# Split transfers, optional zero products and a new step order in an RWKV chunk kernel with a token mixer behind it

## Chip, core and metric

The kernel runs on one core of one Trainium2 chip. Its time is that of one execution on the device in microseconds (us). The core has five engines that run side by side: TensorE (PE in the profile, with its weight loads as PEld) multiplies matrices into PSUM, VectorE (DVE), ScalarE (ACT) and GpSimd (POOL) work on elements, and SyncE (SP) issues transfers. Sixteen DMA engines move the data. POOL does not read PSUM in this kernel; what TensorE makes is taken out by DVE or ACT.

## What is computed

Inputs are r, k, v, w with 4 batches, 8 heads, 768 tokens and 48 channels, u with 8 × 48, and three weight matrices; all in float32. Only the core of the reference is shown:

```python
for t in range(S):                                     # S = 768
    cur = einsum('bhd,bhe->bhde', u[None] * k_t, v_t)
    y[:, :, t] = einsum('bhd,bhde->bhe', r_t, state + cur)
    state = w_t[:, :, :, None] * state + einsum('bhd,bhe->bhde', k_t, v_t)
x = y.transpose(0, 2, 1, 3).reshape(B, S, 384)
W_tok = (1 / 8) * einsum('bsd,btd->bst', x @ w_q, x @ w_k)
out = maximum(einsum('bst,btd->bsd', W_tok, x), 0) @ w_out
```

## The kernel before

The 768 tokens of a batch are three *units* of 256 tokens, each of two chunks (c = 0, 1) of 128. Twelve units, n = 0 to 11, are worked through in turn, three to a batch. Within a chunk the recurrence is written as matrix products. The steps of one unit and their names, which are also tile names in the profile:

- loads of w, k, r, v into wg, kg, rg, vg (rings of four buffers each, 384 KB a load, lines 231 to 240). For the last batch v comes in four pieces vw (line 242).
- **ln** (line 406, ACT): the logarithm of w, into lw. **cw** (line 429, TensorE): its running sums, 16 products with CM. **ep**, **en** (lines 445 and 453, ACT): the exponentials of the sums and of their negatives.
- **k16**, **r16**, **v16** (line 412): casts to bf16, on POOL, ACT or DVE. **kT**, **rT** (line 466, TensorE): their transposes. **ks** (line 501): k out of PSUM. **qT**, **RT** (DVE), **KT** (POOL or DVE; line 519): products with each other and with the exponentials.
- **vp**, **VB** (line 547): v in the chunk order, out of PSUM. **dps**, **dd**, **Vd** (lines 561 to 580): the term with u.
- **A** (line 587, TensorE): the 128 × 128 blocks of all heads of a chunk; **AM** (line 594, DVE): the same with the mask US.
- **kb**, **kd** (lines 602 and 615), **sn**, **SB** (lines 636 to 660): the state. **yi**, **ya** (lines 669 and 680, TensorE) and **X** (line 708, DVE): the output rows.
- **xt**, **XT**, **qk**, **QK**: X transposed and multiplied with w_q and w_k.

After the third unit of a batch come **T**, **TS** (line 791), and for each block of 256 tokens **mx** (line 807), **rl** (the maximum with 0), **fp** (line 825, the product with w_out), **os** (out of PSUM) and **st** (the store, line 840). In unit 0, and at the end, some steps go by single chunks.

`setup` (line 248) clears and builds the constants, with nine products of a zero tile Z on TensorE. `pads` (line 295) clears each of the two kd buffers once. `bonus` (line 374) prepares u: cast uC, transpose uT, copy UB. WARM = 12 (line 139) further products of Z, named z, stand among the steps.

The order is a list: `ORDER` (line 80) names all steps by number, `WAYS` names the engine of each step that has a choice (E, e, c TensorE, the small letters in another form of the same step; A ACT; D, d DVE; P POOL; S SP), and `BANKS` the PSUM bank of each PSUM buffer. The steps are issued in that order; every engine, SP too, takes its own in the order in which they stand, and waits where an operand or a buffer is not ready. The steps named Q and L (line 348, "wire" and "land") have no function and issue nothing.

Of the kernel before, what the change touches and what calls it, by code (L numbers as in the profile page):

```python
# [32 lines left out]
class Plan:  # L33

    ENGINE = dict(E="E", e="E", c="E", A="A", D="D", d="D", P="P", S="S", Q="Q", L="L")

    def __init__(self):
        self.steps = []  # L40
# [20 lines left out]
    def order(self):  # L61
        ways = iter(WAYS)
        for s in self.steps:
            if len(s["ways"]) > 1:
                s["way"] = next(ways)
                assert s["way"] in s["ways"], s["key"]
            s["eng"] = self.ENGINE[s["way"]]
        for b, x in zip(self.banks, BANKS):
            b.bank = x
        assert sorted(ORDER) == list(range(len(self.steps)))  # L70
        done = []
        for i in ORDER:
            s = self.steps[i]
            assert all(x["out"] for x in s["after"]), s["key"]
            if s["buf"] is not None and s["buf"].kind == "x":
                s["buf"].kind = "s" if s["way"] == "E" else "w"
            s["out"] = True
            done.append(s)
        return done


ORDER = [
# [40 lines left out]
]  # L123
WAYS = (
    "PDDDAPPDDdPADPPDDEEEAAPPAdPAAPEAcEEAAPPAPPADPeDEEDAAAAAAAAPPDPDADPeAcEEDAPPAdPAAPEAEEEDA"
    "PPDPPAAPeAEEAAAAAAAAAAPDPPAAPEDEcEAAPPDPPDAPEAEEEAAPPDPPAAPeDceAAAAADADDPAAPPAPEDcEEDAPP"
    "DPPAPeAcceAAPPDPPPAPPAEEDDAEDADAAADAAAADADDA"
)
BANKS = [
# [6 lines left out]
]  # L136


WARM = 12


@with_exitstack
def kernel(
# [12 lines left out]
    nc = tc.nc  # L156
    B, H, S, D = r.shape
# [70 lines left out]
    gv = const([C, 1], F32, "gv")  # L228
    gk = const([C, 1], F32, "gk")

    def load(b, i, tl, ap):
        nc.sync.dma_start(
            out=view(tl, 0, [[D2, H], [1, D2]]),
            in_=ap[b, :, ds(i * U, U)].rearrange("h (p j) d -> p h (j d)", j=2))

    def load_long(b, i, tl, ap):
        nc.sync.dma_start(
            out=view(tl, 0, [[2 * D2, NP], [1, 2 * D2]]),
            in_=dataclasses.replace(ap, offset=(b * H * S + i * U) * D,
                                    ap=[[4 * D, 64], [S * D, H], [1, 4 * D]]))  # L240

    def load_whole(b, q, tl):
        nc.sync.dma_start(
# [102 lines left out]
    wts = {}  # L346

    def dma(key, fn, after=(), buf=None, reads=()):
        x = add(key, "S", fn, after, buf)
        y = add(key + ("wire",), "Q", None, [x])  # L350
        return add(key + ("land",), "L", None, [y], reads=reads)

    def weights():
        def f_qk(e):
# [27 lines left out]
    def unit(n, batch):  # L382
# [9 lines left out]
        for name, ap in (("wg", w), ("kg", k), ("rg", r)) + (() if whole else (("vg", v),)):  # L392
            f = load_long if name in ("kg", "rg") and long else load
            g[name] = ring(name)
            g[name + "L"] = dma((name, n), lambda e, ap=ap, f=f, x=g[name].tile: f(b, i, x, ap),
                                buf=g[name])
            if n == 0 and name == "wg":
                bonus(g["wgL"])
# [404 lines left out]
        for ii in range(NU):  # L803
# [34 lines left out]
                              cols=DM * len(cs), half=-1 if len(cs) > 1 else cs[0])  # L838
            for cs in halves:
                def f_st(e, ii=ii, cs=cs, o=o, q=nc.sync):  # L840
                    q.dma_start(
                        out=out[b, ds(ii * U, U)].rearrange("(p j) d -> p j d", j=2)[
                            :, ds(cs[0], len(cs))],
                        in_=view(o.tile, cs[0] * DM, [[DM, len(cs)], [1, DM]]))
                if end and ii == NU - 1 and cs[0] == 0:
                    add(("st", m, cs[0]), "A", lambda e, f_st=f_st: f_st(e, q=nc.scalar), [oss[cs]],
                        None, [o])
# [8 lines left out]
        unit(n, batch)  # L856
    for x in range(WARM):
        z = bank()
        add(("z", x), "E", lambda e, z=z: mm(at(z), Z[:, ds(0, C)], Z), [], z, [z])

    with tc.manual_schedule():
        setup()
# [31 lines left out]
```

## Time and profile before

| | us |
|---|---|
| median of three runs | 102.27 |
| the runs | 101.17, 102.27, 105.03 |
| span of the profiled execution | 102.5 |
| busy: TensorE | 90.7 |
| busy: VectorE | 84.4 |
| busy: ACT | 79.2 |
| busy: POOL | 69.6 |
| all transfers | 24.68 MB, mean 241 GB/s |

The span is counted from the first to the last instruction on the core. Busy times are sums over all instructions; register, semaphore and transfer-issuing instructions are not among them. Matmuls are pipelined, so a busy TensorE is not one at its peak. The clock that TensorE was granted is given beside each stretch of time, 1.00 being full speed. In a row of the timeline stand the start, the duration, the engine, the line, the operation with the tiles out<-in, the number of instructions merged, and in brackets how long the engine had been idle before and what ended that. The profile's line 179 is the helper that issues every matmul, 327, 329, 333 and 335 are the helper `copy`, 339 and 341 the helper `relu`.

### The profile page before, as it was taken

How to read it: one execution, taken by the hardware profiler on the slowest of the kernel's cores; microseconds unless marked ns; L12 is line 12 of the kernel's file. 1: busy time of each engine (PE TensorE's matmuls, PEld its weight loads, DVE VectorE, ACT ScalarE, POOL GpSimd, SP SyncE). 2: the span in 40 equal slices, each digit the busy share in tenths (PEclk: the TensorE clock that was granted, in tenths of full speed). 3: DMA queues.
4: the chain of work that ended last, by engine and by line, in shares of the span. 5: the costliest groups of instructions: out<-in, count | busy, mean ns of one | idle time of the engine just before them, and what ended most of it. 6: DMA issues, size and time to landing. Idle time of an engine off the chain costs nothing.

```text
span 102.5 us, 4479 instructions
## 1 busy us (share of the span) xinstructions
PE 90.7 (88%) x1902; PEld 65.7 (64%) x1902; DVE 84.4 (82%) x154; ACT 79.2 (77%) x135; POOL 69.6 (68%) x82
## 2 busy tenths in 40 slices
PE   5909899989988999999999999899959999999950
PEld 1205484777677776668786686868748677776610
DVE  6284969857799999989999999999959999784640
ACT  6035779676898799899999999899859976556920
POOL 6866438539998699399999989498996293600000
PEclk9997555555999999999999999999999999999997
DMA  1999999899999999999999999889940037130694
GB/s 34 319 335 344 325 333 238 231 318 335 253 304 291 282 323 323 334 303 240 312 294 307 237 231 188 149 177 279 406 171 6 6 125 287 59 153 6 248 367 156
DMA packets 45141, 24.68 MB, mean 241 GB/s; under 512 B 31552, under 2 KB 43968, under 8 KB 45120
## 3 DMA queue, kind: packets, MB, share of 16 engines
q1 hardware_dynamic: 44960, 24.19, 82.3%
q8 instruction: 15, 0.25, 0.9%
q10 hardware_dynamic: 160, 0.20, 0.5%
q14 instruction: 6, 0.05, 0.1%
HBM read 19.66 MB, written 4.72 MB: 238 GB/s over the span
## 4 chain that ended last, share of the span: by engine, by line
PE 54%; DVE 27%; issue 7%; ACT 6%; POOL 3%; DVEq 0%; POOLq 0%; ACTq 0%
PE PS L179 54%; DVE AM L595 10%; DVE X L710 5%; ACT VB L327 3%; DVE RT L516 2%; DVE ks L333 2%; DVE SB L658 2%; DVE qT L506 2%; DVE kd L298 1%; DVE kd L335 1%; ACT os L327 1%; POOL US L286 1%; POOL CM L268 1%; ACT MX L339 1%; ACT XT L327 1%
## 5 line engine op out<-in xcount | busy, mean ns | idle before, releaser
L595 DVE TENSOR_TENSOR AM<-PS,US 128x1024 bf16<-128x1024 f32 x24 | 28.9, 1218 | 2.8 <-PE PS L179 2.2
L526 POOL TENSOR_TENSOR KT<-ks,en 128x1024 bf16<-128x1024 bf16 (+1 forms) x10 | 19.8, 1979 | 7.3 <-ACT en L454 4.5
L575 POOL TENSOR_TENSOR Vd<-VB,dd 128x768 bf16<-128x768 bf16 (+1 forms) x14 | 18.1, 1292 | 5.9 <-ACT dd L327 3.4
L454 ACT ACTIVATE en<-PS 128x1024 bf16<-128x1024 f32 (+1 forms) x14 | 12.5, 907 | 4.5 <-PE PS L179 4.4
L179 PEld LDWEIGHTS <-KT 48*128 48x128 bf16 (+1 forms) x312 | 10.4, 99 | 6.8 <-issue 5.0
L710 DVE SCALAR_TENSOR_TENSOR X<-PS,gx,Vd 128x384 bf16<-128x384 f32 x22 | 12.5, 610 | 1.7 <-PE PS L179 1.6
L447 ACT ACTIVATE ep<-PS 128x512 bf16<-128x512 f32 (+1 forms) x28 | 13.7, 555 | 0.2 <-ACT dd L327 0.2
L179 PE MATMUL PS<-wo,MX 128*128 128x384 bf16 x72 | 13.5, 326 | 0.0
L407 ACT ACTIVATE lw<-wg 128x768 bf16<-128x768 f32 x12 | 10.2, 853 | 2.7 <-DMA wg<-in_w_dram 2.7
L179 PE MATMUL PS<-RT,KT 48*128 48x128 bf16 x192 | 10.4, 231 | 1.6 <-ACT QK L327 1.1
L179 PE MATMUL PS<-Z 128*128 128x512 bf16 x21 | 9.7, 560 | 1.2 <-DVE Z L250 1.2
L327 ACT COPY os<-PS 128x768 f32<-128x768 f32 (+1 forms) x11 | 7.9, 715 | 2.9 <-PE PS L179 2.8
L418 POOL CAST r<-rg 128x768 bf16<-128x768 f32 x10 | 8.2, 824 | 1.9 <-DMA rg<-in_r_dram 1.9
L179 PEld LDWEIGHTS <-MX 128*128 128x128 bf16 x72 | 6.5, 97 | 3.6 <-DVE MX L341 0.2
L179 PE MATMUL PS<-CM,lw 64*128 64x128 bf16 x192 | 8.2, 231 | 0.6 <-DVE AM L595 0.3
L506 DVE TENSOR_TENSOR qT<-PS,ks 128x1024 bf16<-128x1024 bf16 x12 | 8.2, 684 | 0.5 <-PE PS L179 0.5
L418 POOL CAST k<-kg 128x768 bf16<-128x768 f32 x10 | 8.2, 825 | 0.4 <-DMA kg<-in_k_dram 0.4
L516 DVE TENSOR_TENSOR RT<-PS,ep 128x1024 bf16<-128x1024 bf16 (+1 forms) x14 | 8.4, 605 | 0.0
L339 ACT ACTIVATE MX<-PS 128x768 bf16<-128x768 f32 (+1 forms) x12 | 8.0, 682 | 0.4
L179 PE MATMUL PS<-VB,AM 128*128 128x48 bf16 x192 | 8.3, 188 | 0.0
L658 DVE TENSOR_TENSOR SB<-PS,ep 128x192 bf16<-128x192 f32 x20 | 7.0, 349 | 1.1 <-PE PS L179 1.1
L329 ACT ACTIVATE kd<-PS,gk 128x768 bf16<-128x768 bf16 (+1 forms) x7 | 5.7, 815 | 2.4 <-PE PS L179 2.3
(90 smaller groups left out, 195.6 us busy)
## 6 DMA issues: line engine op xcount, KB each, us to landing
kg<-in_k_dram SPq DMA_DIRECT2D x12, 384.0 KB, 6.1
wg<-in_w_dram SPq DMA_DIRECT2D x12, 384.0 KB, 5.4
rg<-in_r_dram SPq DMA_DIRECT2D x12, 384.0 KB, 5.4
vg<-in_v_dram SPq DMA_DIRECT2D x9, 384.0 KB, 6.4
out_dram<-os SPq DMA_DIRECT2D x9, 384.0 KB, 2.6
vw<-in_v_dram SPq DMA_DIRECT2D x4, 288.0 KB, 7.4
out_dram<-os SPq DMA_DIRECT2D x5, 192.0 KB, 2.4
wof<-in_moe_w_out_dram SPq DMA_DIRECT2D x1, 576.0 KB, 7.1
```

The source lines that it names most:

```text
L179: return nc.tensor.matmul(o, l, rr, start=start, stop=stop, skip_group_check=True, is_transpose=trans)
L327: nc.scalar.copy(o, i)
L407: nc.scalar.activation(view(lw.tile, 0, [[64, H], [512, 2], [1, D]]), view(g["wg"].tile, 0, [[D2, H], [D, 2], [1, D]]), ACT.Ln, bias=0.0, ...
L418: op(view(o.tile, 0, [[64, NP], [256, 4], [1, D]]), view(g[src].tile, 0, [[2 * D2, NP], [D, 4], [1, D]]))
L447: nc.scalar.activation(view(ep.tile, cs[0] * NP * EW + off, [[EW, NP * len(cs)], [step, 2], [1, 32]]), view(at(cw), cs[0] * 512 + j * 64, ...
L454: nc.scalar.activation(en.tile[:, ds(cs[0] * 512, w_)], at(cw)[:, ds(cs[0] * 512, w_)], ACT.Exp, bias=0.0, scale=-1.0)
L506: lambda e: nc.vector.tensor_tensor(plain(qT.tile), turned(512), plain(ks.tile), ALU.mult),
L516: nc.vector.tensor_tensor(plain(RT.tile, cs, 32), turned(512, cs, True), plain(ep.tile, cs, EW // 4), ALU.mult)
L526: x.tensor_tensor(KT.tile[:, cols], ks.tile[:, cols], en.tile[:, cols], ALU.mult)
L575: (nc.vector if e == "D" else nc.gpsimd).tensor_tensor(Vd.tile[:, cols], VB.tile[:, cols], view(dd.tile, cs[0] * H, [[1, len(cs) * H], [0, ...
L595: AMs[c] = add(("AM", n, c), "D", lambda e, c=c, A=A: nc.vector.tensor_tensor(view(AM[c].tile, 0, [[C, 8], [1, C]]), view(at(A), 0, [[C, 8 ...
L710: nc.vector.scalar_tensor_tensor(view(X.tile, 2 * i * DM + hh * D, [[D2, H], [1, D]]), view(at(y), hh * 512, [[D, H], [1, D]]), gx, view(V ...
```

## The change

The lists ORDER, WAYS and BANKS are new, and two kinds of choice are added to them. A load of w, k, r or v and a store may have the way T: it is then issued as two transfers by SP, one of 100 partitions and one of 28. The loads of w of units 3, 7, 8, 9 and 11, the load of k of unit 5 and the stores of blocks 0, 1, 2, 3, 6 and 7 have it. A zero product may have the way N, which issues nothing; of 24 (WARM is 24 now) eight have the way E. The steps "wire" and "land" are gone. The core of the diff:

```diff
-    ENGINE = dict(E="E", e="E", c="E", A="A", D="D", d="D", P="P", S="S", Q="Q", L="L")
+    ENGINE = dict(E="E", e="E", c="E", A="A", D="D", d="D", P="P", S="S", T="S", N="N")
...
-WARM = 12
+WARM = 24
...
-    def load(b, i, tl, ap):
-        nc.sync.dma_start(
-            out=view(tl, 0, [[D2, H], [1, D2]]),
-            in_=ap[b, :, ds(i * U, U)].rearrange("h (p j) d -> p h (j d)", j=2))
+    def pieces(e, n_):
+
+        return [(0, n_)] if e == "S" else [(0, n_ // 32 * 25), (n_ // 32 * 25, n_ // 32 * 7)]
+
+    def load(b, i, tl, ap, e):
+        for p, n_ in pieces(e, 128):
+            nc.sync.dma_start(
+                out=view(tl, 0, [[D2, H], [1, D2]], p0=p, pn=n_),
+                in_=dataclasses.replace(ap, offset=(b * H * S + i * U + 2 * p) * D,
+                                        ap=[[D2, n_], [S * D, H], [1, D2]]))
...
     def dma(key, fn, after=(), buf=None, reads=()):
-        x = add(key, "S", fn, after, buf)
-        y = add(key + ("wire",), "Q", None, [x])
-        return add(key + ("land",), "L", None, [y], reads=reads)
+        return add(key, "ST" if key[0] in ("wg", "kg", "rg", "vg", "st") else "S", fn, after, buf,
+                   reads)
...
-        add(("z", x), "E", lambda e, z=z: mm(at(z), Z[:, ds(0, C)], Z), [], z, [z])
+        add(("z", x), "EN", lambda e, z=z: e == "E" and mm(at(z), Z[:, ds(0, C)], Z), [], z, [z])
```

`load_long` (k and r from unit 1 on) and the store are split in the same way. What the new lists say, read out for the places that matter below (the first number is the unit, the second the chunk; st and fp are counted by blocks):

```text
SP, start       before  kg0 wg0 rg0 vg0 kg1 wg1 rg1 vg1 wg2 kg2 rg2 vg2
                after   wg0 kg0 rg0 wg1 kg1 rg1 vg0 wg2 vg1 kg2 rg2 vg2 wg3/T
SP, end         before  kg10 vw rg10 wg10 vw vw vw kg11 wg11 rg11 st0 st2 st1 st4 st3 st5 st6 st7 ...
                after   wg10 kg9 kg10 rg10 vw vw vw st0/T vw rg11 kg11 st2/T wg11/T st1/T st3/T st5 ...
TensorE, start  before  uT z kT0 cw0 z z rT0 z kb0.0 kb0.1 vp0 kT1 A0.0 dps0 sn0.0 cw1 rT1 sn0.1 z
                        vp1 dps1 A0.1 z z A1.1 kT2 ya0.0 yi0.1 cw2 ya0.1 A1.0 ...
                after   z cw0 kT0 uT z z rT0 z A0.0 cw1 z kT1 rT1 z kb0.0 kb0.1 vp0 z A0.1 dps0 dps1
                        sn0.0 A1.1 kb1 sn0.1 ya0.0 ya0.1 yi0.1 vp1 A1.0 cw2 ...
TensorE, end    before  T11 T11 T11 wq11.1 fp7 mx9 fp8 mx10 fp9.0 fp9.1 mx11 fp10.0 fp10.1 fp11.0 fp11.1 z
                after   fp7 ya11.1 ... T11 T11 T11 wq11.1 fp8 mx9 mx11 mx10 fp9.0 fp9.1 fp10.0 fp11.0
                        fp11.1 fp10.1
DVE, start      before  (setup) pads0 pads1 uC ks0 KT0.0 KT0.1 RT0.0 qT0 kd0.0 RT0.1 kd0.1 AM0.0 ...
                after   (setup) k16-0 pads0 ks0 UB KT0.1 RT0.0 qT0 AM0.0 RT0.1 ks1 qT1 RT1 AM0.1 ...
POOL, start     before  (setup) k16-0 r16-0 v16-0 k16-1 r16-1 v16-1 Vd0.0 ...
                after   (setup) uC pads1 r16-0 KT0.0 k16-1 r16-1 v16-0 KT1 Vd0.0 Vd0.1 ...
POOL, unit 9    before  KT9 KT10 VB9 VB10 Vd9        after  KT9 VB9 KT10 VB10 Vd9
```

Some forty steps change between DVE, ACT and POOL. From unit 3 on, DVE gets VB of 5, XT of 5 and 8, QK of 3 and 8, Vd of 8, dd of 4, 5 and 8 and four of the last rl, and gives up VB of 7, XT of 3, ks of 6, kd of 6, 8 and 9, rl of 7 and several of the last os. kb of units 2, 3, 5 and 8 changes to half as many products of full width, that of unit 6 the other way.

More of the change, by code (lines that the diff above doesn't have):

```diff
@@ L73, in order @@
             s = self.steps[i]
-            assert all(x["out"] for x in s["after"]), s["key"]
+            assert s["way"] == "N" or all(x["out"] for x in s["after"]), s["key"]
             if s["buf"] is not None and s["buf"].kind == "x":
@@ L82 @@
 ORDER = [
[40 rows of a table removed]
[32 rows of a table added]
 ]
 WAYS = (
-    "PDDDAPPDDdPADPPDDEEEAAPPAdPAAPEAcEEAAPPAPPADPeDEEDAAAAAAAAPPDPDADPeAcEEDAPPAdPAAPEAEEEDA"
-    "PPDPPAAPeAEEAAAAAAAAAAPDPPAAPEDEcEAAPPDPPDAPEAEEEAAPPDPPAAPeDceAAAAADADDPAAPPAPEDcEEDAPP"
-    "DPPAPeAcceAAPPDPPPAPPAEEDDAEDADAAADAAAADADDA"
+    "PDPSPDSSSDPDPDPAAPPAAEEEAASSSSPPDPAAAPEAEcEAASSSSPPDdPAAPEAEEDAAAATAATAATTSSSPPDdPADPEAE"
+    "EEADSSSSPPAdPADPEAEEeDASTSSPPDPPDDPEAEEDAAAATAASAASSSSSPPAPPAAPeAEEEAATSSSPPDPPAAPEAEEEA"
+    "ATSSSPPDPPADDEAcEDDAAATAATDASTSSPPAPPAPEAEEEDASSSPPDPPAPeAcEeAATSSPPDPPPAPPAEEDDDEDAAADD"
+    "AASSDDAASSAAADSNEENNNNENNENNNNEENNEENNN"
 )
 BANKS = [
[6 rows of a table removed]
[7 rows of a table added]
 ]
-WARM = 12
+WARM = 24
 @with_exitstack
@@ L229, with load_long @@
     gk = const([C, 1], F32, "gk")
-    def load(b, i, tl, ap):
-        nc.sync.dma_start(
-            out=view(tl, 0, [[D2, H], [1, D2]]),
-            in_=ap[b, :, ds(i * U, U)].rearrange("h (p j) d -> p h (j d)", j=2))
[L236 to L240, printed above, removed]
+    def pieces(e, n_):
[6 more added lines that the diff above has]
+                                        ap=[[D2, n_], [S * D, H], [1, D2]]))
+    def load_long(b, i, tl, ap, e):
+        for p, n_ in pieces(e, 64):
+            nc.sync.dma_start(
+                out=view(tl, 0, [[2 * D2, NP], [1, 2 * D2]], p0=2 * p, pn=2 * n_),
+                in_=dataclasses.replace(ap, offset=(b * H * S + i * U + 4 * p) * D,
+                                        ap=[[4 * D, n_], [S * D, H], [1, 4 * D]]))
     def load_whole(b, q, tl):
@@ L394, in unit @@
             g[name] = ring(name)
-            g[name + "L"] = dma((name, n), lambda e, ap=ap, f=f, x=g[name].tile: f(b, i, x, ap),
+            g[name + "L"] = dma((name, n), lambda e, ap=ap, f=f, x=g[name].tile: f(b, i, x, ap, e),
                                 buf=g[name])
@@ L840, in f_st @@
                 def f_st(e, ii=ii, cs=cs, o=o, q=nc.sync):
[L841 to L844, printed above, removed]
+                    for p, n_ in pieces("T" if e == "T" else "S", 128):
+                        q.dma_start(
+                            out=out[b, ds(ii * U + 2 * p, 2 * n_)].rearrange(
+                                "(p j) d -> p j d", j=2)[:, ds(cs[0], len(cs))],
+                            in_=view(o.tile, cs[0] * DM, [[DM, len(cs)], [1, DM]], p0=p, pn=n_))
                 if end and ii == NU - 1 and cs[0] == 0:
```

85 rows, old and new, of tables (BANKS, ORDER) are left out of this document.

## The prediction

> **What bounds the kernel now.** I read the page first (span, granted clock, the chain that ended last by engine), then the chain piece by piece, then stretches of it by engine.
>
> ```profile
> span 102.5 us, 4479 instructions
> ...
> PEclk9997555555999999999999999999999999999997
> ...
> PE 54%; DVE 27%; issue 7%; ACT 6%; POOL 3%; DVEq 0%; POOLq 0%; ACTq 0%
> ```
>
> TensorE (PE) carries half of the chain and VectorE (DVE) a quarter, and the clock that TensorE was granted is half in six of the 40 slices, early on. The chain of waits says where each engine is last:
>
> ```profile
> 6.88 0.59 DVE kd L298
> 7.47 0.09 DVE uC L333
> ...
> 12.60 9.90 PE PS L179 x160
> ...
> 88.46 10.02 PE PS L179 x107
> ```
>
> So there are four stretches. Up to 7.5 us the end of the chain is VectorE clearing the second kd buffer and then casting uC, for which TensorE waits. From there to about 30 us it is mostly TensorE. Then VectorE is full, and the last 10 us are TensorE again. The stretches by engine:
>
> ```profile
> 5.57:8.98 3.41, 1.38 (x35) 0.98 (x36) 2.31 (x7) 0.60 (x2) 2.07 (x4) 1.00 1.14 336
> 15.81:19.22 3.41, 3.41 (x44) 1.64 (x44) 3.03 (x6) 2.69 (x6) 2.77 (x5) 0.50 0.93 236
> 22.64:26.05 3.41, 3.24 (x43) 2.48 (x44) 2.45 (x4) 2.61 (x5) 3.41 (x3) 0.50 1.09 322
> 56.00:69.50 13.50, 12.69 (x332) 9.60 (x329) 13.50 (x23) 13.14 (x23) 11.77 (x12) 1.00 1.02 205
> ```
>
> The columns are length, then busy time (and count) of PE, weight load, DVE, ACT, POOL, then clock, DMA share and GB/s. The clock falls at the end of the first row and is back at full from the end of the third (26.05 us). Late in the kernel VectorE is busy 13.50 of 13.50 us: there time is saved only by giving it less to do or by bringing it its work earlier.
>
> **The start.** This is the part that I count on. TensorE and the first ACT steps before:
>
> ```profile
> 1.23 4.02 PE L179 MATMUL PS<-Z 128*128 128x512 bf16 x9 [1.23 <-DVE Z L250]
> 7.60 0.17 PE L179 MATMUL PS<-ID,uC 8*128 8x8 bf16 x1 [2.35 <-DVE uC L333]
> ...
> 20.05 1.03 PE L179 MATMUL PS<-CM,lw 64*128 64x128 bf16 x16
> ...
> 27.66 0.62 PE L179 MATMUL PS<-CM,lw 64*128 64x128 bf16 x16
> ```
>
> ```profile
> 5.26 0.84 ACT L407 ACTIVATE lw<-wg 128x768 bf16<-128x768 f32 x1 [2.74 <-DMA wg<-in_w_dram]
> 8.92 1.08 ACT L454 ACTIVATE en<-PS 128x512 bf16<-128x512 f32 x2 [2.81 <-PE PS L179]
> ```
>
> The logarithm ln of unit 0 was done at 6.1 us, but its products cw stood behind uT, and uT behind the wait for uC. In the new order cw is TensorE's second step (after one zero product), uC goes to POOL, and w is loaded ahead of k:
>
> ```profile
> 0.78 0.44 SPq L232 DMA_DIRECT2D kg<-in_k_dram  x1
> 1.28 0.57 SPq L232 DMA_DIRECT2D wg<-in_w_dram  x1
> ```
>
> ```profile
> 6.49 0.83 POOL L421 CAST r<-rg 128x768 bf16<-128x768 f32 x1 [0.53 <-DMA rg<-in_r_dram]
> 7.76 0.83 POOL L333 CAST v<-vg 128x768 bf16<-128x768 f32 x1 [0.45 <-DMA vg<-in_v_dram]
> ...
> 73.48 1.59 POOL L333 CAST VB<-vw 128x768 bf16<-128x768 f32 x2
> ```
>
> Loads land 7.76 − 6.49 = 1.27 us apart. With w first, ln starts between 5.26 − 1.27 = 4.0 and 5.26 − 0.50 = 4.8 us (half a microsecond is what its issue gains); I take 4.4. It ends by 5.3, when TensorE's nine zero products end too; cw (0.62 at full clock) follows by 6.2, and en starts near 6.2 instead of 8.92. The next limit is k: its cast moves to DVE and stands behind the scaling of US, which ends near 6.0; with 0.6 for the cast (POOL's take 0.83), the 0.68 of clearing one kd buffer (0.59 and 0.09 in the chain above), which now stands between and hides the transposes, and 0.68 for the copy ks, POOL can form KT of unit 0 from about 8.0 us, a half of it in 1.0 (the whole is 1.98):
>
> ```profile
> L526 POOL TENSOR_TENSOR KT<-ks,en 128x1024 bf16<-128x1024 bf16 (+1 forms) x10 | 19.8, 1979 | 7.3 <-ACT en L454 4.5
> ...
> L179 PE MATMUL PS<-Z 128*128 128x512 bf16 x21 | 9.7, 560 | 1.2 <-DVE Z L250 1.2
> ...
> L333 DVE COPY ks<-PS 128x1024 bf16<-128x1024 bf16 x8 | 5.5, 683 | 1.0 <-PE PS L179 0.9
> ```
>
> The first product A of unit 0 starts at about 9.1 where it started at 12.60, the head of the long TensorE piece above: 3.5 us ahead. The pads on POOL have no row; a memset of that size took 0.59 us on DVE, casts on POOL 0.83, so 0.6 to 1.2 us. POOL waits for r until 6.49 anyway, which hides it; beyond that every tenth is on the path of RT.
>
> Not all of this survives. v of unit 0 is now the seventh load instead of the fourth, so it lands three slots later, 7.76 + 3 × 1.27 = 11.6 us. Cast 0.83 and the products vp, some 0.5, bring TensorE to about 12.9, and TensorE stands in vp until then, with a zero product, the second A, dps, sn and all of units 1 and 2 queued behind it. From there to the output rows X of unit 0 the new order has 81 products (A 16, dps 16, sn 17, kb of unit 1 8, ya 16, yi 8) and the zero product. The long piece of the chain, 9.90 us for 160, gives 0.062 us for one at half clock, so 5.0, and 0.6 for the zero product: 18.5 us.
>
> ```profile
> 21.62 1.14 DVE L710 SCALAR_TENSOR_TENSOR X<-PS,gx,Vd 128x384 bf16<-128x384 f32 x2 [1.19 <-PE PS L179]
> ```
>
> The lead at X is 21.6 − 18.5 = 3.1 us. If v comes a slot later still it is 1.8; if its lateness costs nothing, 3.5 as for the first A. I take 3.1, the value with every step in it. The PSUM banks are dealt anew, so a product may wait for another copy than before; no row tells which, and these ends take it in.
>
> **The zero products.**
>
> Eight of 24 are switched on, against 12 before, so 21 become 17: 4 × 0.56 = 2.2 us of TensorE time. Three of the four stood late (among units 3 and 7 and at the end), beside a full VectorE or after the last product; nothing for them. The fourth stood in the half-clock stretch and is in the sum above. What they do for the clock is a rival below.
>
> **VectorE's own work.** The new order moves some 40 copies, casts and products between DVE, ACT and POOL. Where VectorE is full, between X of unit 2 and X of unit 11, it gets VB of 5, XT of 5 and 8, QK of 3 and 8, Vd of 8 and three small dd, and gives up VB of 7, ks of 6, kd of 6, 8 and 9 and XT of 3. VB and one XT cancel; four operations of 384 to 1024 columns remain on each side, some 0.7 like ks or shorter, and the three dd are over. I take +0.5 us for it; from −0.5 to +1.5, since QK and Vd in full width have no DVE row here.
>
> **The tail.** Product fp of block 7 moves from behind the last T to in front of it.
>
> ```profile
> 92.45 1.14 PE L179 MATMUL PS<-wo,MX 128*128 128x384 bf16 x6
> ```
>
> It lay on the closing TensorE piece, so at most 1.1 us goes. But TensorE is nearly full ahead of the last T too, so the product costs something in its new place: I take 0.7. The last store still follows the last copy; no change there.
>
> **The split transfers.** A split load goes as 100 partitions over ten DMA engines and 28 over fourteen. A DMA engine handles 8 partitions of a whole load; split, ten of them handle 10 + 2 = 12 if both pieces use the same engines, or 10 if they don't. So a split load holds up the busiest engines by 0.25 to 0.5 of a slot, 0.3 to 0.64 us; six make 1.9 to 3.8 us by the last, and SP issues each twice (0.44 us for the first row above).
>
> ```profile
>   DMA wg<-in_w_dram: 2.7, 1
> ...
> DMA to landing us min/median/max: 4.0/5.4/7.6
> ```
>
> Of w, which five of the six are, ACT waited for one load only, the first, so the rings of four buffers cover it: I cost the loads at nothing. If the cover is gone, each late w stops ln and everything behind it on ACT. The stores are issued among the last loads now, and SP waits there for finished output blocks with the three loads of unit 11 and the last piece of v queued behind; those blocks were copied out long before. Nothing, too. [...]
>
> **Sum.** 102.5 − 3.1 (start) + 0.5 (VectorE) − 0.7 (tail) = 99.2 us. The profiled execution is 0.2 above the median of 102.27, so 99.0 beside the median; I leave the 0.2 out. With the ends of the terms (3.5, −0.5 and 1.1 on one side, 1.8, 1.5 and 0 on the other) it is 97.4 to 102.2. A quarter of its chance lies above 100.2, the bound of 2%, which is about what three runs from 101.17 to 105.03 can tell apart.
>
> **Rivals.** *The lead is lost halfway (0.20): 102.* The last v pieces, vw, feed VB of unit 9. They landed late and slowly:
>
> ```profile
> DMA to landing us min/median/max: 7.0/7.4/7.8
> ```
>
> VB now stands ahead of KT of unit 10 on POOL, at 73.48 − 2.0 (one KT) − 3.1 (lead) = 68.4 us, while a store and the splits' 1.9 to 3.8 us of DMA time stand ahead of the last vw. Where this takes 2.8 us back, 102 remains. Against it: most loads are issued earlier, as buffers come free earlier.
>
> *The half clock lasts longer (0.20): 105.3.* The same 16 products cw took 1.03 us at half and 0.62 at full clock, a factor of 1.66, so 3.41 us at half clock do 2.05 us of work and lose 1.36. The new order uses up seven of its eight zero products by the second A, and only one is left for units 1 and 2. With four or five more such stretches at half clock 99.2 becomes 104.6 to 106.0. It decides from two on: with two, 101.9. For it: the clock did not return on busy time alone (the row from 15.81 is busy 3.41 of 3.41 at 0.50), so the dense zero products may have brought it back. Against it: kb of unit 2 is now in full-width products.
>
> *The clock returns early (0.10): 96.* Seven zero products before 13 us may bring it back by 15.8, three stretches earlier: 3 × 1.36 = 4.1 less for TensorE, of which I let 3.2 through, VectorE being full soon after. [...]
>
> **Chances.** The forecast has 0.50: 0.38 of it faster, 0.12 within 2%. The lost lead gives 0.18 within and 0.02 slower, the long half clock 0.16 slower and 0.04 within, the early clock 0.10 faster. Faster 0.48, within 2% 0.34, slower 0.18. The range is 96.0 to 104.3; the forecast's own is 97.4 to 102.2.
>
> **What would show it.** Right: cw starts before 6.5 us and the first A product before 10, X of unit 0 near 19, VectorE without gaps from 30 us on, and no ACT or POOL wait for a load after 14 us. The start is wrong if A is not before 11; the split's price is wrong if ln or a cast waits for DMA later on; the second rival shows as PEclk 5 beyond slice 10. The forecast fails if the lead at X of unit 2 (33.5 us before) is not there at X of unit 11.

## The result, and the profile after

The changed kernel takes 109.0 us (median of four runs, 108.29 to 110.19) where the kernel before takes 102.31 (101.17 to 105.03): a ratio of 1.067, 95% interval 1.057 to 1.078. It is slower by 6.7 us, and the prediction, 99.2 us, is wrong in sign. Medians and ranges below hold all runs; ratios and their intervals leave disturbed runs out, and where too few were left no ratio is given.

From the page of the changed kernel, its span, the granted clock by slices of 2.7 us, the chain of waits by engine and the group of the logarithm ln:

```profile
span 107.1 us, 4462 instructions
...
PEclk9997555899999999999999859999999999999999
...
PE 36%; DMA 16%; DVE 12%; ACT 10%; POOL 9%; SPq 6%; issue 6%; ACTq 0%; POOLq 0%; DVEq 0%
...
L407 ACT ACTIVATE lw<-wg 128x768 bf16<-128x768 f32 x12 | 10.2, 851 | 5.3 <-DMA wg<-in_w_dram 5.3
```

Transfers now carry 16% of the chain and SyncE's issuing (SPq) 6%; before, neither was in it. The slow clock is shorter than before, half in three slices and again for a moment around 62 us. ACT waits 5.3 us for w where it waited 2.7.

The start, from the timeline of the changed kernel (start, duration, engine, operation, in brackets the idle time and what ended it):

```profile
5.61 0.85 PE L173 MATMUL PS<-CM,lw 64*128 64x128 bf16 x16
...
6.50 1.09 ACT L454 ACTIVATE en<-PS 128x512 bf16<-128x512 f32 x2 [1.38 <-PE PS L173]
...
9.98 0.61 PE L173 MATMUL PS<-RT,KT 48*128 48x128 bf16 x8 [1.14 <-DVE qT L506]
...
19.38 0.62 DVE L710 SCALAR_TENSOR_TENSOR X<-PS,gx,Vd 128x384 bf16<-128x384 f32 x1 [0.66 <-PE PS L173]
```

cw starts at 5.61 us, the first A at 9.98 instead of 12.60 and X of unit 0 at 19.38 instead of 21.62. The start went as foretold. What became of the lead is seen in two windows, each from X of unit 2 to X of unit 11 (columns: length, busy time of PE, weight load, DVE, ACT and POOL, clock, DMA share, GB/s). Before:

```profile
33.50:89.10 55.60, 52.62 (x1314) 40.41 (x1311) 52.90 (x84) 49.73 (x85) 45.82 (x41) 1.00 0.83 231
```

After:

```profile
31.10:94.40 63.30, 55.42 (x1311) 43.33 (x1308) 55.28 (x88) 51.13 (x82) 45.96 (x41) 0.97 0.85 226
```

The 4.6 us between the two spans come apart like this:

| | us |
|---|---|
| X of unit 2 starts at 31.1, not 33.5 | −2.4 |
| VectorE busy from there to X of unit 11: 55.28, not 52.90 | +2.4 |
| VectorE idle there: 63.30 − 55.28 = 8.0, not 55.60 − 52.90 = 2.7 | +5.3 |
| from X of unit 11 to the end: 107.1 − 94.4 = 12.7, not 102.5 − 89.1 = 13.4 | −0.7 |
| sum | +4.6 |

So VectorE got more work, which ate the lead, and stood idle for 5.3 us more. From the waits of the changed kernel by releaser (sum, times, longest), those for loads:

```profile
ACT lw L407 <- DMA wg<-in_w_dram: 5.3, 4, 1.7
...
POOL k L418 <- DMA kg<-in_k_dram: 3.4, 5, 1.1
...
POOL VB L334 <- DMA vw<-in_v_dram: 2.4, 1, 2.4
...
POOL v L334 <- DMA vg<-in_v_dram: 2.2, 3, 1.5
```

Before, the same view has these:

```profile
ACT lw L407 <- DMA wg<-in_w_dram: 2.7, 1, 2.7
...
POOL r L418 <- DMA rg<-in_r_dram: 1.9, 2, 1.6
...
POOL v L333 <- DMA vg<-in_v_dram: 1.1, 3, 0.4
```

The waits of ln after the start are new. The chain of the changed kernel runs through transfers at three places: a piece of k of unit 5, for which the cast on POOL waits, a piece of w of unit 8, for which ln waits, and near 75 us a stretch with stores in it, which ends with the store of block 1, whose buffer a copy os on ACT needs:

```profile
32.14 5.67 DMA kg<-in_k_dram
...
51.32 6.59 DMA wg<-in_w_dram
...
74.60 0.41 SPq L842
...
75.44 0.83 SPq L231
...
76.31 1.69 SPq L231
...
78.05 4.99 DMA out_dram<-os
```

Line 842 is a store and 231 a load: near 75 us SyncE issues the two pieces of the store of block 2, then both pieces of w of unit 11, which the program before had issued at 67.4 us.

A second reading concerns the yardstick. The profiled execution of the changed kernel took 108.85 us and has a span of 107.1: the time of a run is 1.7 us above its span. By that the profiled execution of before, with its span of 102.5, took some 104.2, 2 us more than its median. So the 4.6 us of the table understate the loss of 6.7.

### The profile page after: what moved, and what is told of

It is laid out like the page before. It is cut to its first block, busy times and chain, and to the rows that moved or that the text cites. A ratio compares the mean times of both kernels' runs of the same rounds, so it can differ in the third digit from the quotient of the medians.

```text
span 107.1 us, 4462 instructions
## 1 busy us (share of the span) xinstructions
PE 89.5 (84%) x1882; PEld 66.2 (62%) x1884; DVE 85.5 (80%) x151; ACT 80.3 (75%) x135; POOL 69.9 (65%) x85
## 4 chain that ended last, share of the span: by engine, by line
PE 36%; DMA 16%; DVE 12%; ACT 10%; POOL 9%; SPq 6%; issue 6%; ACTq 0%; POOLq 0%; DVEq 0%
PE PS L173 36%; DMA wg<-in_w_dram 6%; DMA kg<-in_k_dram 5%; DMA out_dram<-os 5%; SPq L231 3%; ACT os L328 3%; DVE X L710 2%; DVE AM L595 2%; SPq L238 2%; POOL KT L526 2%; POOL k L418 2%; ACT MX L340 2%; DVE US L294 1%; POOL Vd L575 1%; ACT en L454 1%
## 5 line engine op out<-in xcount | busy, mean ns | idle before, releaser
L526 POOL TENSOR_TENSOR KT<-ks,en 128x1024 bf16<-128x1024 bf16 (+1 forms) x10 | 18.6, 1865 | 7.3 <-DVE RT L516 2.6
L575 POOL TENSOR_TENSOR Vd<-VB,dd 128x768 bf16<-128x768 bf16 (+1 forms) x13 | 16.5, 1281 | 7.1 <-ACT dd L328 4.3
L173 PE MATMUL PS<-wo,MX 128*128 128x384 bf16 x72 | 13.4, 326 | 1.1 <-DVE X L710 0.7
L328 ACT COPY os<-PS 128x768 f32<-128x768 f32 (+1 forms) x14 | 9.6, 687 | 3.8 <-PE PS L173 3.6
L418 POOL CAST k<-kg 128x768 bf16<-128x768 f32 x11 | 9.1, 829 | 3.4 <-DMA kg<-in_k_dram 3.4
L330 ACT ACTIVATE kd<-PS,gk 128x768 bf16<-128x768 bf16 (+1 forms) x13 | 10.0, 765 | 1.6 <-PE PS L173 1.6
L418 POOL CAST r<-rg 128x768 bf16<-128x768 f32 x11 | 9.1, 830 | 0.2 <-DMA rg<-in_r_dram 0.2
L173 PE MATMUL PS<-VB,AM 128*128 128x48 bf16 x192 | 7.6, 186 | 1.6 <-issue 1.2
L340 ACT ACTIVATE MX<-PS 128x768 bf16<-128x768 f32 (+1 forms) x10 | 7.4, 750 | 1.8 <-PE PS L173 1.8
L334 POOL CAST v<-vg 128x768 bf16<-128x768 f32 x8 | 6.7, 832 | 2.8 <-DMA vg<-in_v_dram 2.2
L328 ACT CAST VB<-PS 128x768 bf16<-128x768 f32 x8 | 6.4, 803 | 2.2 <-PE PS L173 1.9
```

The lines of the kernel that those rows point to most:

```text
L173: return nc.tensor.matmul(o, l, rr, start=start, stop=stop, skip_group_check=True, is_transpose=trans)
L328: nc.scalar.copy(o, i)
L330: nc.scalar.activation(o, i, ACT.Copy, bias=0.0, scale=by)
L340: nc.scalar.activation(o, i, ACT.Relu)
L418: op(view(o.tile, 0, [[64, NP], [256, 4], [1, D]]), view(g[src].tile, 0, [[2 * D2, NP], [D, 4], [1, D]]))
L526: x.tensor_tensor(KT.tile[:, cols], ks.tile[:, cols], en.tile[:, cols], ALU.mult)
```

## The experiments

Every kernel below is built on the changed code; with all transfers whole and the lists of before it issues what the kernel before issued. "Stream" is the sequence of transfers that SyncE issues. Landings are worked out from the landing records of the trace. A whole load leaves sixteen of them, a piece of 100 partitions in the changed kernel ten and one of 28 fourteen; they are read as one for each DMA engine that carries the transfer, and the last one is its landing. A transfer's *slot* is the time from the middle landing of the one ahead of it to its own middle landing, the median over transfers of a kind. The landing of the *last load* of all is 73.4 us before and 82.8 after.

**1. Splits and orders taken apart.** Four kernels. First, the changed kernel with all twelve transfers whole:

```diff
-    st0/T vw rg11 kg11 st2/T wg11/T ...        (wg of 3, 7, 8, 9, 11, kg of 5, six stores: way T)
+    st0 vw rg11 kg11 st2 wg11 ...              (all of them: way S)
```

> The changed kernel with all twelve split transfers whole again; its order, engines and zero products stay. Theory S (the splits put 12 instead of 8 partitions on ten DMA engines, so loads land late and ACT and POOL wait for them): the lead of the start, 2 to 3.7 us up to unit 2, stays, about 99 to 101 us, and the waits of ACT for w (5.3 us) fall below 3. Theory L (the new order of the loads is what makes them late): 106 to 109. Theory C (the new order of the compute steps has waits of its own): 106 to 109, with the waits for loads gone.

Measured: 104.27 us (102.34 to 105.04), with 102.07 for before beside it; no ratio is given. Most of the loss goes with the splits. Whether all of it does stays open: the fastest of the four runs, 102.34, is level with before, the other three are 2 to 3 us above it.

Second, the order of before with the same twelve transfers split:

```diff
-    st0 st2 st1 ...     wg 3, 7, 8, 9, 11, kg 5 and six stores S      (order of before)
+    st0/T st2/T st1/T ...                                          the same T
```

> The kernel before with the same twelve transfers split, everything else as before. S: 106 to 109 us, with waits of ACT for w among the late units. L and C: 102 to 103, since the old order keeps its slack.

Measured: 105.07 us (104.05 to 106.41), ratio 1.030 (1.015 to 1.044). The splits cost about 3 us in the order of before too: they were not free there either.

Third and fourth, the order of the computing steps of one kernel with the order of SyncE's steps of the other, all transfers whole:

```diff
-    TensorE, ACT, DVE, POOL of the new lists, SP of the new lists
+    TensorE, ACT, DVE, POOL of the new lists, SP of the lists of before      (third)
+    TensorE, ACT, DVE, POOL of the lists of before, SP of the new lists      (fourth)
```

> The compute steps in the new order, loads and stores in the old order, nothing split. L: 99 to 101 us. S: no more than the first of these runs, within 1 us of it. C: 106 to 109, as no load order helps.

> The compute steps in the old order, loads and stores in the new order, nothing split. L: 105 to 109 us. S and C: 102 to 103, apart from up to 1 us at the start, where ln of unit 0 is earlier and v of unit 0 later.

Measured: new steps with old transfers 107.96 us (107.4 to 109.31), ratio 1.060 (1.050 to 1.069); old steps with new transfers 105.11 us (104.0 to 107.04), ratio 1.025 (1.012 to 1.037). Neither half is better than the two together (104.27), and the new steps with the old order of loads are clearly worse: the steps and the loads of an order were fitted to each other.

**2. What a split costs.** The changed kernel with even pieces, and with the stores whole:

```diff
-        return [(0, n_)] if e == "S" else [(0, n_ // 32 * 25), (n_ // 32 * 25, n_ // 32 * 7)]
+        return [(0, n_)] if e == "S" else [(0, n_ // 2), (n_ // 2, n_ // 2)]
```

> The changed kernel with the same twelve transfers in two pieces each, but of 64 and 64 partitions, which lie on sixteen DMA engines each, so that no engine has more than 8. If the split costs by the ten engines that carry both pieces: 103.5 to 105.5 us, as with whole transfers (104.3). If it costs by the second issue and the second completion: 107.5 to 109.5, as changed (109.0).

Measured: 107.86 us (107.44 to 108.22), ratio 1.063 (1.053 to 1.072).

```diff
-    st0/T st1/T st2/T st3/T st6/T st7/T
+    st0 st1 st2 st3 st6 st7
```

> The changed kernel with the six loads split and the six stores whole. If the late loads are the price: 107 to 109 us, close to the changed kernel, with more of the difference to 104.3 than half. If the stores among the last loads are the price: 104 to 106.

Measured: 106.17 us (105.19 to 107.51), ratio 1.037 (1.024 to 1.050). With the stores whole, the median is 2.8 us below that of the changed kernel and 1.9 above that of the kernel with all transfers whole. This run speaks on the clock as well:

```profile
core 0: 103.5 us, clock 1.000
```

The clock was full, and still VectorE, in the same window from unit 2 to unit 11, was idle for 61.70 − 55.08 = 6.6 us:

```profile
28.90:90.60 61.70, 53.66 (x1305) 41.76 (x1303) 55.08 (x89) 51.64 (x84) 45.82 (x41) 1.00 0.87 236
```

Later, a third way to cut, 112 and 16 partitions (`n_ // 8 * 7` and `n_ // 8`):

> The changed kernel with the same twelve transfers split as 112 and 16 partitions instead of 100 and 28, so that both pieces are spread over sixteen DMA engines evenly (7 and 1 partitions each). Theory 1 (a second transfer costs the stream by itself): a split load still holds it about 1.9 us, 107 to 109. Theory 2 (pieces that touch few partitions, or few engines, are the slow ones, and the piece of 112 runs like a whole load): 1.2 to 1.4 us a load, and the time near the 104.3 of the kernel with whole transfers, 104 to 105.5.

Measured: 105.95 us (104.75 to 108.51), ratio 1.034 (1.022 to 1.046), between the two theories. (Not quite as the expectation has it, the k load of unit 5 goes over fourteen and eight engines by the count of its landings; the other eleven are even.) The slots, in us, first piece and second, from these traces:

| | load of w | store ahead of 80 us |
|---|---|---|
| whole | 1.20 | 0.94 |
| 112 + 16 | 1.44 + 0.23 | 0.96 + 0.20 |
| 64 + 64 | 0.99 + 0.87 | 0.54 + 0.51 |
| 100 + 28 | 1.74 + 0.23 | 1.48 − 0.10 |

By these medians a load cut as 100 and 28 holds the stream for 1.97 us instead of 1.20, and cut as 112 and 16 or as 64 and 64 it still costs 0.5 to 0.7 us more than whole: the second transfer by itself has a price. How much the uneven cut adds is not shown. The medians are of five loads or three to four stores, and single ones spread widely: whole loads of the order of before from 1.13 to 1.80 us, 64 + 64 from 1.60 to 2.27, 112 + 16 from 1.39 to 2.40, 100 + 28 from 1.81 to 2.56. The whole stores have 0.94 in the order of before and 1.28 in the first kernel of experiment 1, so the 1.38 of a split store is rougher still.

**3. Stores among the last loads.** The new order, all transfers whole, with two stores moved:

```diff
-    wg10 kg9 kg10 rg10 vw vw vw st0 vw rg11 kg11 st2 wg11 st1 st3 ...
+    wg10 kg9 kg10 rg10 vw vw vw vw rg11 kg11 wg11 st0 st2 st1 st3 ...
```

> The new order with nothing split and the stores of blocks 0 and 2 moved behind the last load, as in the kernel before. If these two stores, 1.2 to 1.3 us of transfer each ahead of the last loads of v, r, k and w, make what is left between 104.3 and 102.1: 102 to 103 us, the last load landing 2 to 3 us earlier. If the new compute order does: 104 to 105.

Measured: 102.54 us (102.06 to 105.72, ten runs), ratio 1.010 (1.004 to 1.015). It is the best kernel with the new order, and no better than before. Beside the 104.27 (102.34 to 105.04) of the first kernel, whose four runs overlap with these, the two stores cost 1.7 us or nothing; this stays open.

**4. The start alone.** The order of before with only the new start: w of unit 0 loaded ahead of k, uC on POOL, one zero product and cw ahead of kT and uT:

```diff
-    SP kg0 wg0 ...    TensorE uT z kT0 cw0 ...    DVE pads0 pads1 uC ks0 ...
+    SP wg0 kg0 ...    TensorE z cw0 kT0 uT ...    DVE pads0 pads1 ks0 ...      POOL uC k16-0 ...
```

> The kernel before with its start changed alone: w loaded ahead of k, uC cast on POOL, and on TensorE a zero product and cw ahead of kT and uT. cw should start near 5.6 us instead of 8.3. If a lead at the start lasts to the end: 100 to 101 us. If the stream of loads sets the pace of the middle (the last load lands at 73.4 us whatever the start): 101.5 to 103.

Measured: 103.91 us (101.66 to 104.71), with 102.05 for before beside it; no ratio is given. No gain is to be seen. cw did start at 5.61 us and the first A at 10.48, but in a profiled execution with half clock from 10.31 to 13.73 and from 17.14 to 23.97 us, and X of unit 2 starts at 33.3 us, where it did before.

**5. Has the stream slack?** The order of before with six whole loads less, and with six more:

```diff
     def load(b, i, tl, ap, e):
+        if e == "T":
+            return
```

where the loads of w of units 4, 5, 7, 8, 9 and 11 have way T.

> Order of before, with all transfers whole; the loads of w of units 4, 5, 7, 8, 9 and 11 are left out, so the logarithm of those units reads the w of the unit four earlier and the output is another one. Theory 1 (the stream of loads sets the pace in the middle): six slots of about 1.2 us go, so the loads behind them land up to 7 us earlier and the time falls by 2 to 4 us, until TensorE's own 90 us of work bound it: 98 to 100. Theory 2 (the engines set the pace and loads only follow as buffers come free): within 1 us of before, 101 to 103.

Measured: 101.27 us (100.36 to 102.19), ratio 0.985 (0.977 to 0.994): a gain of 1 to 1.5 us, against the 2 to 4 of theory 1. Each load taken away is worth 0.3 us at most.

```diff
+    spare = [const([C, HW], F32, f"spare_{x}") for x in range(2)]
...
     def load(b, i, tl, ap, e):
-        for p, n_ in pieces(e, 128):
+        for t in [tl] if e == "S" else [tl, spare[len(turn) % 2]]:
...
```

> Order of before, with all transfers whole; right behind each load of w of units 4, 5, 7, 8, 9 and 11 the same 384 KB are loaded once more into a spare buffer that nothing reads. Theory 1 (no slack in the stream): six slots of 1.2 us more, 7 us more at the last load, of which 4 to 7 us show: 106 to 109; a split load of 0.7 us more is then about half of this. Theory 2 (the stream has slack, and the splits cost through something else): within 1.5 us of before, 101 to 104.

Measured: 110.16 us (108.12 to 110.54), with 102.22 beside it; no ratio. It is 6 to 8 us slower, so each load added costs 1.0 to 1.3 us, its whole slot. So the order of before stands near the point where the engines and the stream are equally long: six more loads do not go into the stream for free, and little is won by taking six from it.

Then the same six loads left out of the new order with the stores behind:

> The new order, all transfers whole, the stores of blocks 0 and 2 behind the last load, and the loads of w of units 4, 5, 7, 8, 9 and 11 left out as in the run with the order of before. Theory 1 (the stream ate the start's lead): with the stream relieved the lead of 3 to 4 us at X of unit 0 reaches the end, so it is 2 to 4 us faster than the order of before with the same loads left out. Theory 2 (the new order of the computing steps itself gives the lead back): no faster than that, within 1 us or slower.

Measured: 101.84 us (100.0 to 104.46), ratio 0.992 (0.986 to 0.997). The order of before with the same loads left out has 101.27, as theory 2 has it: even with a relieved stream the new order keeps nothing of its lead. The two windows, X of unit 2 to X of unit 11, without these loads, order of before and then new order:

```profile
30.60:84.80 54.20, 52.54 (x1309) 40.45 (x1309) 52.87 (x85) 49.30 (x84) 46.28 (x41) 1.00 0.76 205
```

```profile
28.20:87.90 59.70, 54.69 (x1302) 42.54 (x1299) 55.32 (x89) 51.87 (x84) 46.57 (x42) 0.97 0.74 211
```

The new order is 30.6 − 28.2 = 2.4 us ahead at unit 2 (its clock was full until 51.3 us, the other had half clock from 8.5 to 11.9) and then needs 5.5 us more: 55.32 − 52.87 = 2.5 of work of VectorE and 3.0 of idle time, part of it in a stretch of half clock at 51.3 us.

**6. VectorE's work.** In the window VectorE has, by groups, these operations in the new order (the kernel of experiment 3; the changed kernel has the same counts), which it did not have before:

```profile
L571 DVE TENSOR_TENSOR Vd<-VB,dd 128x768 bf16<-128x768 bf16 x1 | 2.1, 2071 | 0.0
L330 DVE CAST QK<-PS 128x384 bf16<-128x384 f32 x2 | 1.1, 548 | 0.0
```

and before it had these, which the new order gives to ACT:

```profile
L335 DVE TENSOR_SCALAR kd<-PS,gk 128x768 bf16<-128x768 bf16 x2 | 1.2, 606 | 0.0
...
L335 DVE TENSOR_SCALAR kd<-PS,gk 128x384 bf16<-128x384 bf16 x1 | 0.4, 418 | 0.0
```

Taking Vd of unit 8 and QK of units 3 and 8 off VectorE in the new order, and putting them on it in the order of before:

```diff
-    Vd8 D   QK3 D   QK8 D        (new order, stores behind the loads)
+    Vd8 P   QK3 A   QK8 A
```

```diff
-    Vd8 P   QK3 A   QK8 A        (order of before)
+    Vd8 D   QK3 D   QK8 D
```

> The new order, all transfers whole, stores of blocks 0 and 2 behind the last load; in addition Vd of unit 8 goes back to POOL and QK of units 3 and 8 back to ACT, at their places. Theory 1 (these three on a full VectorE take the lead back): VectorE is busy about 52 us instead of 55.1 between X of unit 2 and X of unit 11, that stretch is 2 to 3 us shorter, and the time is 1.5 to 3 us below the same kernel without this edit, 99.5 to 101, which is below before. Theory 2 (the order does it): VectorE stands idle for what it no longer works, and the time stays at 102 to 103.

> The order of before, all transfers whole, with Vd of unit 8 on VectorE instead of POOL and QK of units 3 and 8 on VectorE instead of ACT, at their places. Theory 1: VectorE is busy 3 us more between X of unit 2 and X of unit 11, and the time rises by 2 to 3 us to 104 to 105. Theory 2: within 1 us of before.

Measured, with 101.55 us for before: the order of before with the three on VectorE 105.01 us (104.4 to 106.62), ratio 1.034 (1.024 to 1.043), the time that theory 1 named. VectorE is busy 56.26 us from unit 2 to unit 11, 3.4 more than the 52.90 of before. Not all of the time need be VectorE's: this execution has half clock from 66.8 to 73.7 us, and at a mean clock of 0.967 the kernel took 104.4 and 104.71, the order of before at 0.966 and 0.967 between 101.55 and 103.74.

The new order with VectorE relieved took 107.09 us (106.31 to 108.1), ratio 1.057 (1.050 to 1.064): against theory 1, and worse than theory 2. Its window, and rows of POOL and VectorE near the place:

```profile
30.10:93.00 62.90, 55.05 (x1310) 42.75 (x1306) 52.10 (x84) 52.12 (x84) 47.05 (x42) 0.97 0.81 226
```

```profile
71.24 1.47 POOL L571 TENSOR_TENSOR Vd<-VB,dd 128x768 bf16<-128x768 bf16 x1
72.75 1.14 DVE L706 SCALAR_TENSOR_TENSOR X<-PS,gx,Vd 128x384 bf16<-128x384 f32 x2 [3.42 <-POOL Vd L571]
...
74.63 2.13 POOL L522 TENSOR_TENSOR KT<-ks,en 128x1024 bf16<-128x1024 bf16 x1 [1.92 <-PE PS L169]
```

VectorE is busy 3.0 us less than the 55.11 of the same kernel without the edit, and idle 10.8. Of this, 3.4 us are the wait of X of unit 8 for its Vd, which on POOL stands behind KT and VB of unit 9. KT of unit 10, next behind Vd on POOL, starts at 74.63; without the edit it stood at 71.65 of its span:

```profile
71.65 2.13 POOL L522 TENSOR_TENSOR KT<-ks,en 128x1024 bf16<-128x1024 bf16 x1 [1.24 <-DVE ks L330]
```

It does not wait for Vd: POOL is idle for 1.92 us before it, until TensorE is done. So the run does not test a relieved VectorE alone. It gave Vd a place on POOL at which X has to wait for it, and its result says nothing against theory 1. That is not the whole lag either: X of unit 5 already stood at 51.5 us against 49.8 without the edit, and there is a stretch of half clock from 74.9 us.

The 2.07 us of Vd on VectorE are not all work. In the changed kernel:

```profile
72.55 2.13 POOL L526 TENSOR_TENSOR KT<-ks,en 128x1024 bf16<-128x1024 bf16 x1 [2.38 <-ACT ks L328]
...
73.42 2.07 DVE L575 TENSOR_TENSOR Vd<-VB,dd 128x768 bf16<-128x768 bf16 x1
```

KT on POOL ends at 74.68, Vd 0.81 us later. In all nine executions with a Vd on VectorE such a KT was under way on POOL when it began, and Vd's time less what the two have in common is 0.81 us each time (2.07 − 1.26 here; 2.32 − 1.51 in the order of before). So it looks as if Vd stood still until KT had ended.

**All profiled executions in one table.** Landing of the last load and span, both of the same execution, in us:

| order of before | last load | span | new order | last load | span |
|---|---|---|---|---|---|
| six loads fewer | 67.0 | 98.6 | six loads fewer, stores behind | 65.3 | 100.7 |
| before | 73.4 | 102.5 | whole, stores behind | 74.8 | 100.6 |
| new start alone | 75.7 | 102.2 | whole | 76.5 | 103.3 |
| twelve splits | 77.8 | 102.3 | loads split | 79.0 | 103.5 |
| six loads more | 82.5 | 106.4 | 112 + 16 | 79.6 | 104.2 |
| | | | 64 + 64 | 81.2 | 106.5 |
| | | | changed kernel | 82.8 | 107.1 |

From 74.8 to 82.8 us the spans of the new order rise with the last load, by (107.1 − 100.6) / (82.8 − 74.8) = 0.8 us for each us. Below that the table says little, since the execution with six loads fewer took 102.43 us where the median of its runs is 101.84. The table alone does not tell cause from effect either, because SyncE also waits for buffers that the engines free (1.9 us ahead of one k load in the changed kernel). The direction is shown by the runs in which nothing but transfers was changed: with the twelve splits both orders lose, and six loads more cost 6 to 8 us.

Of the 8.0 us by which the changed kernel's last load is later than that of the kernel with the stores behind, 6.3 go with the splits (82.8 − 76.5) and 1.7 with the place of two stores. How the 6.3 divide between loads and stores is not shown. With the stores whole the last load lands at 79.0, 3.8 us earlier, but 3.6 of these are there at X of unit 7, before a split store can have had an effect. The changed kernel, then the one with whole stores:

```profile
69.22 1.25 SPq L842 DMA_DIRECT2D out_dram<-os  x1
69.69 1.13 DVE L710 SCALAR_TENSOR_TENSOR X<-PS,gx,Vd 128x384 bf16<-128x384 f32 x2
```

```profile
66.09 1.13 DVE L706 SCALAR_TENSOR_TENSOR X<-PS,gx,Vd 128x384 bf16<-128x384 f32 x2
67.21 1.47 SPq L838 DMA_DIRECT2D out_dram<-os  x1
```

Up to there both issue the same transfers, and the second ran at full clock. The row of before stands high for its long half clock. The two kernels with crossed lists (74.5 and 106.2; 78.9 and 105.3) and those of the sixth experiment lie off this line: in them other things than the last load are late.

## Why the prediction was wrong, step by step

- **The yardstick.** "The profiled execution is 0.2 above the median" set a span against a time. The difference of time and span, 1.7 us, had to be added, and the execution profiled was 2 us above its median, with a half clock of 17 us. The 99.2 of the sum is a span; as a time it is 100.9.
- **The start, −3.1.** Right in mechanism, too large in size. 19.38 us for X of unit 0 gives 2.2, and 2.4 are there at unit 2, but a part of this is the long half clock of the execution before. The cast of k on VectorE, estimated at 0.6 us, took 1.64, beside the clearing of a kd buffer on POOL. In executions with one half-clock stretch of 3.4 us before 20 us, X of unit 0 starts at 19.5 in the order of before (six loads fewer) and at 18.1 in the new one (stores behind), X of unit 2 at 30.6 and 29.8: a lead of 1.4, then 0.8.
- **VectorE's own work, +0.5.** The term was mis-sized: 2.4 us, outside its range of −0.5 to 1.5. One Vd, 2.07 us on VectorE, is most of it. It was counted as one "like ks or shorter", 0.7, and the 0.81 that are left of it beside KT come near that. What the sum did not have is that it was put where KT runs on POOL, which added 1.26.
- **The tail, −0.7.** Right: 13.4 us became 12.7.
- **The split transfers, nothing.** This is the step that turned the sign: the splits cost 3 us in the order of before (105.07 against 102.07) and most of the loss in the new one (109.0 against 104.27 with all whole). The cover named was that "ACT waited for one w load only, the first". That ACT waited for none later showed that loads arrived in time, not by how much. Six loads more cost 6 to 8 us in the same order: the margin was next to nothing. The price itself was also too low, 0.77 us a load (1.97 − 1.20) where the upper end had 0.64, because the second transfer costs something of its own: 0.47 us a load cut as 112 and 16, 0.66 as 64 and 64. The estimate's other ground, that both pieces use the same engines, fits the one load looked at, though no record names an engine. Of the fourteen landings of the 28-partition piece of w of unit 11, four come at 79.50 to 80.00 us and ten from 81.08 on, as they would if four of its engines had no part in the piece of 100 ahead of it, which has ten landings. (An earlier record at 78.19, 0.2 us behind the end of the issue, is left out.) The splits are not all that was wrong: with all transfers whole the new order takes 104.27 us, or 102.54 with the stores behind, not less than before. There the lead was lost as well, to VectorE's added time and to idle time whose cause stays open.
- **The stores, "Nothing, too".** The answer looked only at whether the blocks were ready. Their slots were left out: a split store takes about 1.4 us of the stream, two of them stand ahead of w of unit 11, and the chain of the changed kernel runs through them at 75 us. With all six stores whole the median is 2.8 us lower. By their slots the two stores ahead of w would explain some 0.9 of this (2 × 0.44), and what the rest is stays open.
- **The zero products, nothing.** No run tried them by themselves. The clock, which they might have served, was not the cause: a run of the changed kernel at a mean clock of 0.984 took 108.29 us, the runs of the order of before at 0.983 took 100.71 to 102.82.
- **The rivals.** The lost lead was the right direction and had one right place. POOL's VB of unit 9 waits for v:

```profile
77.11 0.82 POOL L334 CAST VB<-vw 128x768 bf16<-128x768 f32 x1 [2.43 <-DMA vw<-in_v_dram]
```

  It was priced as one late piece, 2.8 us; the whole stream was late. The longer half clock did not come: 10 us near the start instead of 17, and 3.4 later. The kernel with only loads split ran at full clock, and at 105.19 us it was still slower than before. The early clock came in part, at 19.8 us instead of 26.05 (the rival had 15.8), and no gain of it is left at the end.
- **What would show it.** The lead at unit 2 was there and gone at unit 11 (94.4 against 89.1), the mark set for failure; ln and the casts waited for transfers, the mark set for a wrong price of the split.

What stays open: how much of the remaining idle time in the new order, 3 us in the kernel with six loads fewer, is due to its steps and how much to the clock; how the cost of the splits divides between loads and stores; and how much of a split's price is the uneven cut.

## What to carry to other kernels

That nobody waits for a transfer says nothing about its slack: before costing a transfer's extra time at nothing, find when each load lands and when it is needed, in the stretch where the kernel is fullest. The orders of work and of loads in a step list are fitted to each other, so a part of it, good or bad, can't be priced or moved alone. When an operation moves to another engine, look at what it will stand behind there and at what runs beside it. And set a profiled span against the time of the same execution, since a long execution makes any lead at the place where it lost time look real.

## What the runs showed of the hardware

A load of 384 KB cut in two held the stream longer, however it was cut: 1.97 us (100 + 28), 1.86 (64 + 64) and 1.67 (112 + 16) against 1.20 whole, as medians.

SyncE can be held at an issue: in the changed kernel the issues of two pieces of w took 3.05 us with no other engine named for a wait, where one issue at the start took 0.62. At most five transfers were under way at such times. A long issue can also be a wait for a buffer: of the 2.38 us of one k load, 1.9 were for Vd on POOL.

```profile
54.80 3.05 SPq L231 DMA_DIRECT2D wg<-in_w_dram  x2
```

```profile
34.96 2.38 SPq L238 DMA_DIRECT2D kg<-in_k_dram  x1
```

```profile
SPq L238 <- POOL Vd L575: 1.9, 1, 1.9
```

And one Vd of 128 × 768 in bf16, with no operand in PSUM, took VectorE 2.07 us beside a KT on POOL that had started before it, 0.81 of them after the end of that KT; alone on POOL a Vd takes 1.48.
